# Alternating the two tokens of an output block in PSUM, and storing every other partition

## The chip, the cores and the metric

The kernel runs on one core of a Trainium2 chip. The metric is the time of one execution on the device in microseconds, as the median of several runs. TensorE (PE) does the matrix products into PSUM, ScalarE (ACT) and VectorE (DVE) read PSUM and write SBUF, GpSimd (POOL) works on SBUF alone, and SyncE (SP) issues most DMAs.

## The reference

An efficient attention over 8 batches, 8 heads, 576 tokens and 64 features a head is followed by a multiplicative feed-forward network without a nonlinearity, so that w3 and w_out can be folded into one matrix:

```python
q_s = softmax(q, axis=-1); k_s = softmax(k, axis=2)
kv = einsum('bhsd,bhse->bhde', k_s, v)
attn = einsum('bhsd,bhde->bhse', q_s, kv)
x = attn.transpose(0, 2, 1, 3).reshape(B * S, H * D)      # 4608 x 512
out = (((x @ w1) * (x @ w2)) @ w3) @ w_out                # 4608 x 512, float32
```

## The kernel before, in words

The order of all instructions is a list written out in the file (ORDER), and another list (PICKS) says on which engine a step runs. The steps are recorded in that order, and every engine runs its own share of it as a queue.

**A batch.** q, k and v of one batch lie in SBUF with 128 partitions = 2 groups of heads x 64 token groups; token group p holds the 9 consecutive tokens 9p to 9p + 8, numbered j = 0 to 8. The softmaxes run on ScalarE, VectorE and GpSimd, and kv is a set of small matmuls (L580). The normalised q is transposed, by TensorE or (step qd, L680) by a DMA, into qT, whose columns are ordered by j and then by the 64 groups c.

**The product of q and kv** (prod, L697 to L709). It makes x transposed: features on partitions, tokens along the columns. The first 512 columns (j = 0 to 7) are the main part (tiles named xm, in the pools att, po and pab; the profile names a tile by its pool or by its first use), the last 64 (j = 8) the tail (xt), which is collected over all batches. A matmul here uses a 64x64 quarter of the array: i picks 64 rows of it and one PSUM bank, gg picks 64 columns of it and one half of the partitions. Batches 0 and 1 (SPLIT) make the main part in two halves of 256 columns with two pairs of heads each; batches 2 to 7 make one pair of heads at a time over all 512 columns. The result is scaled and cast to float16 in x by ScalarE or VectorE (xs, L711). The column t of x is token j = t // 64 of group c = t % 64.

**The network.** For a chunk of 512 columns the two up products (L851, or L939 by a seven-product scheme in chunks 6 to 8) are multiplied into ab, and the down product gives 128 tokens x 512 (L873) in chunks 0 and 1. In chunks 2 to 8 (SEVEN) the seven-product scheme (L1029) gives blocks of 2 x 128 tokens and 256 columns. Chunk 8 is the tail of all batches. A block of 128 tokens, number tb, has the columns 128 tb to 128 tb + 127 of x on its partitions: in the first 64 partitions the tokens j = 2 tb of the 64 groups, in the last 64 the tokens j = 2 tb + 1.

**The stores.** The blocks are copied or added into osb (four buffers; in chunks 7 and 8 other tiles that have come free, which the profile names k and v) and stored from there. store (L910) issues two DMAs of 64 partitions x 2 KB for each block of chunks 0 and 1. store_block (L1056) issues two DMAs of 64 partitions x 2 x 1 KB for each block of chunks 2 to 7; in chunk 7 (TWOQ) one of them goes from ScalarE's queue, all others from SP's. For chunk 8 it issues DMAs of all 128 partitions. A buffer of osb is given back when its stores have landed.

Of the kernel before, what the change touches and what calls it, by code (L numbers as in the profile page):

```python
# [265 lines left out]
def kernel(  # L266
# [11 lines left out]
    nc = tc.nc  # L278
    B, H, S, D = q.shape
# [7 lines left out]
    HALF = P // G  # L287
    HH = H // G
    NHP = HH // 2
    NJ = S // HALF  # L290
# [27 lines left out]
    def p_att(shape, dtype, name):  # L318
        return att_pool.tile(shape, dtype, tag="att", name=name)
# [5 lines left out]
    st = {}  # L325
# [195 lines left out]
    def attention(b):  # L521
# [119 lines left out]
        def qeps(p, eng):  # L641
            rr = st["qr", b][:, :, slice(*PARTS[p])]
            if eng == "ACT":
                nc.scalar.activation(out=rr, in_=rr, func=AF.Identity, bias=epst[:, 0:1])
            else:
                return [dve.tensor_scalar_add(out=rr, in0=rr, scalar1=EPS)]
# [35 lines left out]
        def toks(i, hp, gg, j0, j1):  # L682

            return st["qT", b].rearrange("p (j a) (g c) -> p j a g c", a=NHP, g=G)[
                i * D:(i + 1) * D, j0:j1, hp, gg, :]

        def xtile():
            if ("x", b) not in st:
                st["x", b] = work.tile([P, N_CT, MAIN], F16, tag="x", name="x", bufs=NX)
            return st["x", b]  # L690

        def XRING(name):
            if name[1] < XMS:
                return "att"
            return "pab" if name[0] == "xt" else "po" if name[2] else "att"

        def prod(name, hp_list, j0, j1, dst):  # L697
            n = (j1 - j0) * HALF
            for i in range(2):
                bank = {"att": lambda: p_att([P, 512], F32, name[0]), "po": p_o, "pab": p_ab}[XRING(name)]()  # L700
                st[(*name, i)] = bank[:, 0:len(hp_list) * n].rearrange("p (a n) -> p a n", n=n)
            for a, hp in enumerate(hp_list):
                for i in range(2):
                    for gg in range(G):
                        nc.tensor.matmul(  # L705
                            st[(*name, i)][gg * D:(gg + 1) * D, a, :].rearrange(
                                "p (j c) -> p j c", c=HALF),
                            lhsT=st["kv2", b][i * D:(i + 1) * D, hp, gg, :],
                            rhs=toks(i, hp, gg, j0, j1), start=True, stop=True)  # L709

        def xs(name, i, dst, eng):  # L711
            scale(eng, dst(), st[(*name, i)], SC)
# [22 lines left out]
        for p in parts:  # L735
            n = (PARTS[p][1] - PARTS[p][0]) * HH * D
# [6 lines left out]
              lambda eng, p=p: qeps(p, eng), [("qsm", b, p)])  # L743
# [24 lines left out]
        if len(SUBS[b]) == 2:  # L768
            for h in range(2):
                name = ("xm", b, h)  # L770
                dst = lambda i, h=h: xtile()[:, i::2, h * 256:(h + 1) * 256]
                A(name, "PE", 0.22, lambda name=name, h=h: prod(name, [0, 1], 4 * h, 4 * h + 4, None),
                  kvs + qready(h) + free, takes=XRING(name), slots=2, slack=SLACK)
                for i in range(2):
                    A(("xs", b, h, i), moves(512), 0,
                      lambda eng, name=name, i=i, dst=dst: xs(name, i, lambda: dst(i), eng), [name],
                      gives=[name])
            last = [("xm", b, 1)]
            XS[b] = [[("xs", b, h, i) for i in range(2)] for h in range(2)]
        else:  # L780
            for hp in hps:
                name = ("xm", b, hp)
                A(name, "PE", 0.22, lambda name=name, hp=hp: prod(name, [hp], 0, NM, None),
                  kvs + qready(0) + qready(1) + free, takes=XRING(name), slots=2, slack=SLACK)
                for i in range(2):
                    A(("xs", b, hp, i), moves(512), 0,
                      lambda eng, name=name, i=i, hp=hp: xs(
                          name, i, lambda: xtile()[:, 2 * hp + i:2 * hp + i + 1, :], eng),
                      [name], gives=[name])
            last = [("xm", b, hp) for hp in hps]  # L790
            XS[b] = [[("xs", b, hp, i) for hp in hps for i in range(2)]]
        A(("xt", b), "PE", 0.07, lambda: prod(("xt", b), [0, 1], NM, NJ, None), last + qready(1),
          takes=XRING(("xt", b)), slots=2, slack=SLACK)
        for i in range(2):
            A(("xts", b, i), moves(128), 0,
              lambda eng, i=i: xs(("xt", b), i, lambda: xtail[:, i::2, b * HALF:(b + 1) * HALF], eng),
# [40 lines left out]
    def chunk(c):  # L837
# [68 lines left out]
        def os2(tb, c0, c1, eng):  # L906
            st["osb", c, tb, c0] = obuf(c1 - c0)
            copy(eng, st["osb", c, tb, c0], st["po", c, tb, c0][:, 0:c1 - c0])

        def store(tb):  # L910
            for i in range(2):
                b, j = c, 2 * tb + i
                nc.sync.dma_start(
                    out=out[b * S:(b + 1) * S, :].rearrange("(p j) c -> p j c", j=NJ)[:, j, :],
                    in_=st["osb", c, tb][i * HALF:(i + 1) * HALF, :])

        def x_sum(i, eng):
            x0, x1 = [x()[:, 0:2, t:t + 256] for t in (0, 256)], [x()[:, 2:4, t:t + 256] for t in (0, 256)]
            b11, b12, b21, b22 = x0[0], x0[1], x1[0], x1[1]
            s = xsums(c)  # L920
            in0, in1 = {1: (b12, b11), 2: (b22, s[0]), 3: (b22, b12), 4: (b21, s[1])}[i]
            return [engine[eng].tensor_tensor(out=s[i - 1], in0=in0, in1=in1, op=ALU.subtract)]
# [79 lines left out]
        def sums_of(i, eng):  # L1002
            a = st["ab", c]
            a11, a12, a21, a22 = [a[:, 4 * f:4 * f + 4, 256 * t:256 * t + 256]
                                  for t in range(2) for f in range(2)]
            in0, in1, op = {1: (a21, a22, ALU.add), 2: (mine[0], a11, ALU.subtract),
                            3: (a11, a21, ALU.subtract), 4: (a12, mine[1], ALU.subtract)}[i]
            return [engine[eng].tensor_tensor(out=mine[i - 1], in0=in0, in1=in1, op=op)]  # L1008
# [47 lines left out]
        def store_block(n, part=None, z=None):  # L1056
            t0, c0 = n // 10 - 1, (n % 10 - 1) * 256
            if part is not None:
                (nc.sync if part else nc.scalar).dma_start(
                    out=out.rearrange("(t p j) c -> p t j c", p=P, j=NJ)[  # L1060
                        :, 2 * t0 + part, NM, c0:c0 + 256],
                    in_=st["osb", c, n][:, 256 * part:256 * part + 256])
                return
            if c == B:
                nc.sync.dma_start(
                    out=out.rearrange("(t p j) c -> p t j c", p=P, j=NJ)[
                        :, 2 * t0:2 * t0 + 2, NM, c0:c0 + 256],
                    in_=st["osb", c, n].rearrange("p (t x) -> p t x", t=2))
                return
            for i in range(2) if z is None else (z,):  # L1070
                j = 4 * t0 + i
                (nc.scalar if z else nc.sync).dma_start(
                    out=out[c * S:(c + 1) * S, :].rearrange("(p j) c -> p j c", j=NJ)[
                        :, j:j + 3:2, c0:c0 + 256],
                    in_=st["osb", c, n][i * HALF:(i + 1) * HALF, :].rearrange(
                        "p (t x) -> p t x", t=2))

        A = plan.add
        nf = len(SUBS[c])
# [7 lines left out]
        if c in UPS + UP1:  # L1087
# [15 lines left out]
            for i, needs in ((1, []), (2, [("xd", c, 1)]), (3, []), (4, [("xd", c, 2)])):  # L1103
                A(("xd", c, i), {"POOL": (1.06, True), "DVE": (0.39, True)}, 0,
                  lambda eng, i=i: x_sum(i, eng), needs + xn + held)
            for g in range(2):
                for one in kinds:
                    k = lambda i: ("vk", one, c, g, i)
                    p = lambda i: ("vp", one, c, g, i)
# [12 lines left out]
                    for n, needs, gives in (  # L1122
# [8 lines left out]
                        b = ("bs", c, sub, u)  # L1131
# [33 lines left out]
        if c in SEVEN:  # L1165
# [8 lines left out]
            for i, needs in ((3, lo), (1, lo + hi), (2, [("sa", c, 1)]), (4, [("sa", c, 2)])):  # L1174
                A(("sa", c, i), {"POOL": (1.9, True), "DVE": (0.69, True)}, 0,
                  lambda eng, i=i: sums_of(i, eng), needs + last)
# [42 lines left out]
        for sub in range(nf):  # L1219
            for tb in range(4):  # L1220
# [18 lines left out]
                for c0, c1 in zip(cuts, cuts[1:]):  # L1239
# [4 lines left out]
                      lambda eng, tb=tb, c0=c0, c1=c1: os2(tb, c0, c1, eng), [("down", *it)] + gone,  # L1244
# [6 lines left out]
    def weight_sum(i, eng):  # L1251
        b11, b12, b21, b22 = [W3O[:, 4 * f:4 * f + 4, 256 * x:256 * x + 256]
                              for f in range(2) for x in range(2)]
        in0, in1 = {1: (b12, b11), 2: (b22, sums[0]), 3: (b22, b12), 4: (b21, sums[1])}[i]
        return [engine[eng].tensor_tensor(out=sums[i - 1], in0=in0, in1=in1, op=ALU.subtract)]

    for i, needs in ((1, []), (2, [("sT", 1)]), (3, []), (4, [("sT", 2)])):
        plan.add(("sT", i), {"POOL": (1.9, True), "DVE": (0.69, True)}, 0,
                 lambda eng, i=i: weight_sum(i, eng),
# [48 lines left out]
```

## Time and profile before

| what | value |
|---|---|
| median of 3 runs | 230.78 us (230.62 to 231.79) |
| the profiled execution | 231.41 us |
| its span, first to last instruction | 229.6 us |
| granted TensorE clock | 1.000 |
| DMA packets | 42201, 46.56 MB |
| of them under 512 B | 17088 |
| HBM written | 9.44 MB |

The span is what the rows of the profile cover; the rest of the execution's time lies around it. In rows of groups the columns are the source line, engine, operation, output and inputs with their shapes, then the count, the busy time in us, the mean of one in ns and the idle time of the engine ahead of it. Matmuls overlap in TensorE's pipeline, so the duration of one is longer than the distance from its start to the next.

### The profile page before, as it was taken

How to read it: one execution, taken by the hardware profiler on the slowest of the kernel's cores; microseconds unless marked ns; L12 is line 12 of the kernel's file. 1: busy time of each engine (PE TensorE's matmuls, PEld its weight loads, DVE VectorE, ACT ScalarE, POOL GpSimd, SP SyncE). 2: the span in 40 equal slices, each digit the busy share in tenths (PEclk: the TensorE clock that was granted, in tenths of full speed). 3: DMA queues.
4: the chain of work that ended last, by engine and by line, in shares of the span. 5: the costliest groups of instructions: out<-in, count | busy, mean ns of one | idle time of the engine just before them, and what ended most of it. 6: DMA issues, size and time to landing. Idle time of an engine off the chain costs nothing.

```text
span 229.6 us, 5583 instructions
## 1 busy us (share of the span) xinstructions
PE 220.3 (96%) x2239; PEld 149.1 (65%) x2239; DVE 202.6 (88%) x313; ACT 146.4 (64%) x277; POOL 144.1 (63%) x93
## 2 busy tenths in 40 slices
PE   7789999999999999999999999999999999999993
PEld 2345658765857635345665665664788788888882
DVE  1997769989897999999999899899989999899982
ACT  0536865479964899968947889448578453344521
POOL 8233337909999987994895895643099335638200
PEclk9999999999999999999999999999999999999999
DMA  6999999999999979999892866872803430041537
GB/s 201 219 310 210 294 264 264 312 382 295 394 311 215 358 259 222 283 302 301 246 386 76 179 139 176 330 150 47 183 3 76 97 74 1 3 91 27 113 91 229
DMA packets 42201, 46.56 MB, mean 203 GB/s; under 512 B 17088, under 2 KB 29888, under 8 KB 42176
## 3 DMA queue, kind: packets, MB, share of 16 engines
q1 hardware_dynamic: 33920, 33.82, 53.0%
q0 software_dynamic: 7536, 11.73, 21.8%
q10 hardware_dynamic: 720, 0.66, 1.0%
q8 instruction: 17, 0.28, 0.5%
q14 instruction: 8, 0.07, 0.1%
HBM read 38.80 MB, written 9.44 MB: 210 GB/s over the span
## 4 chain that ended last, share of the span: by engine, by line
PE 72%; DMA 22%; issue 1%; POOL 1%; ACT 1%; DVE 0%; POOLq 0%; ACTq 0%
PE pab L851 27%; PE po L1029 16%; PE pg L939 9%; PE pab L939 7%; DMA q<-in_q_dram 6%; DMA k<-in_k_dram 6%; PE po L873 6%; DMA w1sb<-in_moe_w_dram 5%; DMA v<-in_v_dram 4%; PE pab L1029 2%; PE pkv L580 2%; PE xm L705 1%; POOL w L450 1%; PE po L705 0%; POOL wosb L450 0%
## 5 line engine op out<-in xcount | busy, mean ns | idle before, releaser
L851 PE MATMUL pab<-x,w1sb 128*128 128x256 f16 (+1 forms) x256 | 49.5, 326 | 0.3 <-DMA w1sb<-in_moe_w_dram 0.3
L851 PE MATMUL pab<-x,w2sb 128*128 128x256 f16 (+1 forms) x256 | 49.5, 326 | 0.0
L555 POOL TENSOR_TENSOR k<-k,cb 128x1152 f32<-128x1152 f32 x13 | 34.1, 2634 | 14.7 <-DVE w L1008 8.6
L851 PEld LDWEIGHTS <-w1sb 128*128 128x128 f16 x256 | 24.5, 98 | 15.1 <-DMA w1sb<-in_moe_w_dram 0.6
L851 PEld LDWEIGHTS <-w2sb 128*128 128x128 f16 x256 | 24.2, 98 | 15.2 <-issue 1.1
L866 DVE TENSOR_TENSOR ab<-pab,bsb 128x512 f16<-128x512 f32 x48 | 31.8, 676 | 2.0 <-ACT bsb L366 1.2
L625 POOL TENSOR_TENSOR q<-q,qm 128x1280 f32<-128x1280 f32 (+1 forms) x13 | 27.8, 2144 | 4.8 <-issue 2.3
L366 ACT CAST bsb<-pab 128x512 f16<-128x512 f32 x37 | 21.7, 585 | 12.6 <-PE pab L851 12.1
L657 POOL TENSOR_TENSOR en<-eq,qr 128x1024 f16<-128x1024 f16 (+1 forms) x12 | 25.4, 2124 | 6.5 <-ACT bsb L366 5.0
L620 DVE TENSOR_REDUCE qm<-q 128x20 f32<-128x1280 f32 (+1 forms) x16 | 21.3, 1339 | 3.9 <-DMA q<-in_q_dram 3.9
L638 DVE TENSOR_REDUCE qr<-eq 128x20 f32<-128x1280 f16 (+1 forms) x16 | 21.5, 1341 | 1.6 <-ACT eq L633 1.5
L633 ACT ACTIVATE eq<-q 128x1280 f16<-128x1280 f32 (+1 forms) x16 | 18.6, 1167 | 5.3 <-DVE q L625 3.9
L1029 PEld LDWEIGHTS <-w 128*128 128x128 f16 x192 | 18.6, 98 | 4.1 <-issue 0.4
L532 DVE TRANSPOSE_TENSOR_REDUCE kt<-k 128x72 f32<-128x2304 f32 x8 | 20.6, 2570 | 0.1
L366 ACT COPY q<-pg 128x512 f32<-128x512 f32 x19 | 10.8, 586 | 13.9 <-PE pg L939 7.7
L1029 PEld LDWEIGHTS <-ab 128*128 128x128 f16 x168 | 16.4, 98 | 3.5 <-issue 0.2
L563 ACT ACTIVATE ek<-k 128x1152 f16<-128x1152 f32 x16 | 18.3, 1165 | 0.0
L1029 PE MATMUL po<-w 128*128 128x256 f16 x144 | 18.0, 273 | 0.0
L1008 POOL TENSOR_TENSOR w<-ab 128x1024 f16<-128x1024 f16 x5 | 10.6, 2125 | 9.7 <-PE pg L939 3.7
L501 PE MATMUL po<-wosb,w3T 128*128 128x512 f16 x64 | 15.3, 379 | 0.6 <-DMA wosb<-in_moe_w_out_dram 0.5
L873 PE MATMUL po<-W3O,ab 128*128 128x512 f16 x64 | 15.1, 379 | 0.5 <-ACT osb L366 0.5
L366 ACT CAST v<-v 128x1152 f16<-128x1152 f32 x12 | 13.6, 1156 | 2.0 <-DMA v<-in_v_dram 2.0
(145 smaller groups left out, 425.2 us busy)
## 6 DMA issues: line engine op xcount, KB each, us to landing
out_dram<-osb SPq DMA_DIRECT2D x56, 128.0 KB, 2.6
q<-in_q_dram SPq DMA_DIRECT2D x5, 1152.0 KB, 8.0
v<-in_v_dram SPq DMA_DIRECT2D x5, 1152.0 KB, 7.2
k<-in_k_dram SPq DMA_DIRECT2D x4, 1152.0 KB, 9.5
k<-in_k_dram POOLq DMA_DIRECT2D x3, 1152.0 KB, 14.3
v<-in_v_dram POOLq DMA_DIRECT2D x1, 1152.0 KB, 14.0
q<-in_q_dram SPq DMA_DIRECT2D x2, 576.0 KB, 5.8
k<-in_k_dram SPq DMA_DIRECT2D x2, 576.0 KB, 5.0
```

What stands on the lines that cost most here:

```text
L366: return [(nc.scalar.copy if eng == "ACT" else engine[eng].tensor_copy)(out=out, in_=in_)]
L532: dve.tensor_reduce(out=st["kt", b].rearrange("p h j e -> p (h j e)"), in_=kb.rearrange("p h j (e c) -> p (h j e) c", c=QD), axis=AX.X, op ...
L555: return [engine[eng].tensor_tensor(out=kb[:, two(hp), :, :], in0=kb[:, two(hp), :, :], in1=st["cb", b][:, two(hp), None, :].broadcast_to( ...
L620: dve.tensor_reduce(out=st["qm", b][:, :, j], in_=qb[:, :, j, :], axis=AX.X, op=ALU.max)
L625: return [engine[eng].tensor_tensor(out=qb[:, :, j, :], in0=qb[:, :, j, :], in1=st["qm", b][:, :, j, None].broadcast_to([P, HH, n, D]), op ...
L638: dve.tensor_reduce(out=st["qr", b][:, :, slice(*PARTS[p])], in_=st["eq", b, p], axis=AX.X, op=ALU.add)
L657: return [engine[eng].tensor_tensor(out=st["en", b][:, j, :, :].rearrange("p j h d -> p h j d"), in0=st["eq", b, p], in1=st["qr", b][:, :, ...
L851: nc.tensor.matmul(st["p", one, c, sub, u][:, a * (t1 - t0):(a + 1) * (t1 - t0)], lhsT=w[:, ct, fb * P:(fb + 1) * P], rhs=x()[:, ct, t0:t1 ...
L866: dve.tensor_tensor(out=st["ab", c][:, nf * u:nf * u + nf, t0:t1], in0=cut(st["p", 0, c, sub, u]), in1=cut(st["bsb", c, sub, u]), op=ALU.mult)
L873: nc.tensor.matmul(st["po", c, tb], lhsT=st["ab", c][:, ft, tb * P:(tb + 1) * P], rhs=W3O[:, ft, :], start=(ft == 0), stop=(ft == N_FT - 1))
L939: nc.tensor.matmul(st["pg", one, c, g, bank][:, a * 256:a * 256 + 256], lhsT=t[:, c0 + ct, f:f + P], rhs=r[:, r0 + ct, t0:t0 + 256], start ...
L1029: nc.tensor.matmul(to, lhsT=t[:, f0 + ft, t0 + tb * P:t0 + tb * P + P], rhs=r[:, g0 + ft, c0:c0 + 256], start=fresh and (tb == 0 or wide_) ...
```

## The change

TensorE's main products write the columns of a block in another order. Of each four values of j (4h to 4h + 3), j = 4h + 2z + t goes to block 2h + t, and there to the partitions 2c + z. So a block holds the tokens j and j + 2 of the 64 groups alternating, one token of a group on the even partition and the other on the odd one. In PSUM the 64 columns of one j, which were side by side, are 2 fp32 elements apart; the moving operand is read as before, and a matmul's output, 64x512 before, has the form 64x2x2x128 (64x2x128 for the halves of 256). The tail products are written as before.

The stores follow: one DMA takes the even partitions of a block and one the odd ones, in place of the first 64 and the last 64. In store_block the two tokens of a DMA are now j and j + 1, where they were j and j + 2. The sizes, the number of DMAs and the queues stay. On all five engines the instructions stand in the same order as before.

```diff
@@ prod
                     for gg in range(G):
+                        to = st[(*name, i)][gg * D:(gg + 1) * D, a, :]
                         nc.tensor.matmul(
-                            st[(*name, i)][gg * D:(gg + 1) * D, a, :].rearrange(
-                                "p (j c) -> p j c", c=HALF),
+                            to.rearrange("p (j c) -> p j c", c=HALF) if name[0] == "xt" else
+                            to.rearrange("p (h t c z) -> p h z t c", t=2, z=2, c=HALF),
                             lhsT=st["kv2", b][i * D:(i + 1) * D, hp, gg, :],
                             rhs=toks(i, hp, gg, j0, j1), start=True, stop=True)
@@ store
-            for i in range(2):
-                b, j = c, 2 * tb + i
+            for z in range(2):
+                j = tb // 2 * 4 + tb % 2 + 2 * z
                 nc.sync.dma_start(
-                    out=out[b * S:(b + 1) * S, :].rearrange("(p j) c -> p j c", j=NJ)[:, j, :],
-                    in_=st["osb", c, tb][i * HALF:(i + 1) * HALF, :])
+                    out=out[c * S:(c + 1) * S, :].rearrange("(p j) c -> p j c", j=NJ)[:, j, :],
+                    in_=st["osb", c, tb][z::2, :])
@@ store_block
-            for i in range(2) if z is None else (z,):
-                j = 4 * t0 + i
-                (nc.scalar if z else nc.sync).dma_start(
+            for z, queue in ((0, nc.sync), (1, nc.sync)) if z is None else ((z, (nc.sync, nc.scalar)[z]),):
+                j = 4 * t0 + 2 * z
+                queue.dma_start(
                     out=out[c * S:(c + 1) * S, :].rearrange("(p j) c -> p j c", j=NJ)[
-                        :, j:j + 3:2, c0:c0 + 256],
-                    in_=st["osb", c, n][i * HALF:(i + 1) * HALF, :].rearrange(
-                        "p (t x) -> p t x", t=2))
+                        :, j:j + 2, c0:c0 + 256],
+                    in_=st["osb", c, n][z::2, :].rearrange("p (t x) -> p t x", t=2))
```

## The prediction

> **What bounds the kernel now.** I read the busy shares first, then the same by stage, then what TensorE waits for, then the chain that ended last, and only then the lines that the change touches. The page gives the shares of the whole span:
>
> ```profile
> PE 220.3 (96%) x2239; PEld 149.1 (65%) x2239; DVE 202.6 (88%) x313; ACT 146.4 (64%) x277; POOL 144.1 (63%) x93
> ```
>
> An average hides stages, so the next view cuts the span. Its columns are the stretch, its length, then busy time and count of each engine, the granted clock, the share of the 16 DMA engines and GB/s:
>
> ```profile
> 31.00:46.00 15.00, 14.66 (x139) 11.21 (x139) 13.70 (x18) 7.33 (x16) 12.34 (x9) 1.00 1.30 278
> 46.00:100.00 54.00, 53.18 (x566) 31.35 (x565) 49.39 (x72) 44.63 (x85) 45.67 (x23) 1.00 1.01 307
> 100.00:160.00 60.00, 60.00 (x604) 35.65 (x603) 56.98 (x87) 44.94 (x94) 41.52 (x19) 1.00 0.75 207
> 160.00:226.00 66.00, 65.82 (x667) 56.69 (x664) 60.45 (x108) 33.29 (x60) 31.57 (x20) 1.00 0.34 75
> ```
>
> From 46 to 226 us TensorE is busy 179.0 of 180.0 us, at the full clock. The DMA engines are full up to 100 us (1.01), then 0.75, then 0.34. Full DMA engines alone would not bound; what decides is whether TensorE waits for them. All of TensorE's waits from 46 us on:
>
> ```profile
> PE po L873 <- ACT osb L366: 0.5, 1, 0.5
> PE pab L851 <- DMA w1sb<-in_moe_w_dram: 0.3, 1, 0.3
> PE xm L705 <- DMA qT<-en: 0.3, 1, 0.3
> PE po L1029 <- ACT x L370: 0.2, 1, 0.2
> ```
>
> Four waits, 1.3 us together. No wait for a store stands here. So a transfer that becomes faster can give back part of 1.3 us at most, while every 0.1 us more of TensorE's own work in this stretch moves the end by nearly 0.1 us. The chain of waits says the same at its end (start, length, what):
>
> ```profile
> 92.31 1.73 PE pab L851 x8
> ...
> 95.19 0.34 PE xm L705 x4
> 95.53 0.22 PE po L705 x4
> ...
> 145.12 0.87 PE po L1029 x8
> ...
> 222.51 3.09 PE pab L1029 x28
> ```
>
> L705, the matmuls that the change alters, stands in it as a link of its own.
>
> **The change, part 1: TensorE's writes.** No instruction is added, removed or moved on any engine; the order of all five is the same. What differs on TensorE is where the columns of L705 land: in the main products two neighbouring columns of the moving operand now land two fp32 elements (8 bytes) apart in PSUM instead of side by side. The tail products (xt) keep their form. How many there are, from the view of L705:
>
> ```profile
> L705 PE MATMUL xm<-qT,kv x60: 267/293/401, 31.1 to 182.1; 64*64 64x256 f16 x32, 64*64 64x512 f16 x28
> ...
> L705 PE MATMUL xt<-qT,kv x24: 192/203/214, 34.6 to 94.0; 64*64 64x64 f16 x24
> L705 PE MATMUL po<-qT,kv x20: 372/389/400, 95.4 to 181.8; 64*64 64x512 f16 x20
> ```
>
> That is 48 matmuls of 512 columns (28 + 20) and 32 of 256. They do not cost their durations one after another: each takes a 64x64 quarter of the array, and the four of a set run together. The timeline shows two such sets:
>
> ```profile
> 95.12 0.41 PE L705 MATMUL xm<-qT,kv 64*64 64x512 f16 x4
> 95.36 0.39 PE L705 MATMUL po<-qT,kv 64*64 64x512 f16 x4
> ```
>
> The four of the first start in one merged row at 95.12 and the next set starts 0.24 us later. A full-array matmul of 512 columns takes 1.73 / 8 = 0.216 us in the chain's row at 92.31, one of 256 columns 0.87 / 8 = 0.109 us in the row at 145.12. So a set costs one pass of its columns, and there are 12 sets of 512 (6 batches of 2) and 8 sets of 256 (batches 0 and 1).
>
> Nothing in this trace writes PSUM from TensorE with a step, so the price has to be bounded. From below: a column costs what it costs now, 0.216 / 512 = 0.42 ns, and the price is nothing. From above I take the other engines that touch PSUM, one element of each partition at a time:
>
> ```profile
> L366 ACT COPY osb<-po 128x512 f32<-128x512 f32 x10 | 5.9, 585 | 2.9 <-PE po L1029 2.9
> L370 ACT ACTIVATE xtail<-pab 128x128 f16<-128x128 f32 x8 | 2.0, 282 | 0.0
> L366 DVE COPY osb<-po 128x512 f32<-128x512 f32 x3 | 2.1, 687 | 1.2 <-PE po L873 0.7 <-PE po L1029 0.6
> L372 DVE TENSOR_SCALAR xtail<-pab 128x128 f16<-128x128 f32 x2 | 0.6, 283 | 0.0
> ```
>
> The slope between 128 and 512 elements is (585 - 282) / 384 = 0.79 ns an element on ScalarE, and (687 - 283) / 384 = 1.05 ns on VectorE. TensorE puts a value into each partition every 0.42 ns, about twice as fast as either. The simplest reading is that TensorE's neighbours go in as a pair, and that a value whose neighbour goes elsewhere takes the place of a pair. Then a set takes two passes. That lies nearest to ScalarE's 0.79 ns (0.79 / 0.42 = 1.9), and it is the value that I take:
>
> - 12 sets x 0.216 = 2.59 us; 8 sets x 0.109 = 0.87 us; together 3.46 us more of TensorE.
> - At ScalarE's slope: 12 x (0.404 - 0.216) + 8 x (0.202 - 0.109) = 3.0 us. At VectorE's: 12 x (0.538 - 0.216) + 8 x (0.269 - 0.109) = 5.1 us. These and zero are the ends.
>
> Behind a longer set stand the casts to x on ScalarE and VectorE, which wait for it, and the next matmuls in TensorE's queue, which have no other work to hide it: TensorE was busy through. Only the waits can absorb something. The 0.3 us for w1sb ends with a weight load, and the transposed load of qT with a DMA behind the softmax; neither is timed by TensorE, so both absorb what reaches them: 0.6. The 0.5 us for ScalarE's osb is the open one. ScalarE's queue ahead of it:
>
> ```profile
> 79.26 1.16 ACT L366 CAST v<-v 128x1152 f16<-128x1152 f32 x1 [0.63 <-DMA v<-in_v_dram]
> ...
> 80.32 0.58 ACT L366 CAST bsb<-pab 128x512 f16<-128x512 f32 x1
> ...
> 81.97 0.57 ACT L366 COPY osb<-po 128x512 f32<-128x512 f32 x1
> ```
>
> The cast of v is timed by a load, the cast bsb takes a product from TensorE, and osb stands behind both; so the wait may move along with TensorE (absorbs 0) or stay (absorbs 0.5); I take half. The 0.2 us for x comes right behind L705 itself and moves with it: 0. Net: 3.46 - 0.6 - 0.25 = **2.6 us**, with 2.2 (all 1.3 absorbed) and 2.9 as its own ends.
>
> [...]
>
> **Part 2: the stores.** Each 128 KB store reads 64 partitions, before as one half, now as every other one; the number of DMAs, their bytes and their runs in DRAM stay. What the store packets cost shows in two windows of the DMA view, the first from 201 to 204 us with half-partition stores alone, the second from 226.00 to 228.25 us with the last stores, over 128 partitions (packets, MB, share of 16 engines):
>
> ```profile
> q1 hardware_dynamic: 568, 0.52, 82.5%
> ```
>
> ```profile
> q1 hardware_dynamic: 623, 0.60, 79.8%
> q10 hardware_dynamic: 144, 0.13, 17.8%
> ```
>
> 0.825 x 16 x 3 us / 568 = 70 ns a packet against 0.976 x 16 x 2.25 us / 767 = 46 ns. If every other partition gives the second figure, a store of 128 packets takes 0.37 us of the 16 engines instead of 0.56. What is that worth? When the stores are issued, from the view of osb:
>
> ```profile
> L1072 SPq DMA_DIRECT2D out_dram<-osb x40: 595/602/652, 124.5 to 212.3; - x40
> L913 SPq DMA_DIRECT2D out_dram<-osb x16: 512/595/2826, 51.5 to 114.1; - x16
> ```
>
> The 40 run after 124 us, where the DMA engines have a share of 0.75 and less and nobody waits for a store; SP itself needs 0.60 us to issue one, longer than either figure: 0 us. The 16 earlier ones (whole rows of 2 KB) share full DMA engines with loads; what they free can come back only through the 1.3 us of waits. The tail stays: the chain runs on matmuls to 225.6 us, then the last VectorE block and the last stores, which belong to the tail chunk and are not changed. I take 0, with -0.8 (the qT and osb waits gone) as the lower end.
>
> [...]
>
> **Sum.** The profiled execution took 231.41 us with a span of 229.6. Its sum is 231.41 + 2.6 = 234.0. The median of the runs is 230.78, 0.63 below that execution, so I forecast 230.78 + 2.6 = **233.4**.
>
> **Rivals.**
> - **The step is free.** TensorE's write keeps its 0.42 ns whatever the address. For it: nothing in the trace shows a stepped write to be slow, and the pair is an inference from other engines. Then nothing remains: 230.8, within 230.4 to 231.2.
> - **The other side: faster.** The step is free, and the lighter stores let loads land earlier between 46 and 100 us, so that the qT wait and the osb wait go: 0.3 + 0.5 = 0.8 us, 230.0. Against it: those waits end with a transpose behind the softmax and with ScalarE, whose queue held a cast of v that a load released; only that one has a DMA behind it. It decides only if the step costs less than 0.8 us in all, which is 0.05 us for a set of 512.
> - **A stepped value costs as much as on VectorE** (1.05 ns). 5.1 - 0.85 = 4.3 us: 235.1. For it: it is the slowest access of PSUM in the trace. Against it: ScalarE does better on the same banks.
> - **A partial price**, some set-up per set rather than per column: between 231.2 and 232.6.
>
> **How the numbers follow.** Two passes (with ScalarE's slope) 0.60, its own range 232.8 to 233.8; free 0.25; faster 0.05; VectorE's price 0.06; partial 0.04. A measurement of this kernel tells about 0.5% (1.15 us) from no change. Free lies within it, and so does a quarter of partial (0.01): same 0.26. Faster: I leave its whole 0.05, though it reaches only 230.0. Slower: 0.60 + 0.06 + 0.03 = 0.69. The range goes from 230.3, which takes in the free case, to 235.1, the upper bound of the unknown price.
>
> **What would show it.** If I am right, the start of the second set of L705 moves from 0.24 to about 0.45 us behind the first, the chain's 0.34 + 0.22 for a batch becomes about 1.0, the durations of the 512 forms go from 390 to about 600 ns while xt keeps its 203, the waits for w1sb and qT vanish, and the last matmul ends 2.6 us later than now. The half-partition stores show about 46 ns a packet and nobody is earlier for it. If the sets keep their 0.24, the step is free and the forecast is wrong in its first term. If the sets double and the end does not move, the error is in what the waits absorb. If waits for a load appear or vanish by more than 0.8 us, part 2 was misjudged.

## The result, and the profile after

The changed kernel takes 233.18 us (median of 6 runs, 232.93 to 233.74) against 230.74 us for the kernel before in the same comparison. The ratio is 1.0102, 95% interval 1.0081 to 1.0124: 2.4 us slower, 1.9 to 2.9. The profiled execution took 233.22 us with a span of 231.4.

The page's first line, of the kernel after: TensorE has 3.1 us more of busy time, no other engine has moved by more than 0.5 us.

```profile
PE 223.4 (97%) x2239; PEld 149.5 (65%) x2239; DVE 202.8 (88%) x313; ACT 146.9 (63%) x277; POOL 144.0 (62%) x93
```

The same cut into stretches (length, then busy time and count of each engine, granted clock, share of the DMA engines, GB/s):

```profile
31.00:46.00 15.00, 15.00 (x138) 11.22 (x137) 13.22 (x18) 6.75 (x16) 11.52 (x9) 1.00 1.30 279
46.00:100.00 54.00, 54.00 (x568) 31.34 (x566) 49.83 (x72) 45.36 (x86) 46.13 (x23) 1.00 0.98 309
100.00:160.00 60.00, 60.00 (x599) 35.22 (x597) 56.33 (x86) 43.96 (x92) 41.84 (x19) 1.00 0.69 203
160.00:226.00 66.00, 66.00 (x659) 56.28 (x658) 60.75 (x107) 34.17 (x62) 31.55 (x20) 1.00 0.24 70
```

TensorE is now busy without a gap from 31 to 226 us: the four waits of before, 1.3 us, are gone, and the list of its waits after 46 us is empty. The DMA engines have less to do after 100 us (0.69 and 0.24, before 0.75 and 0.34), and nobody gained by it.

The lines that the change altered. First the groups of L706 (the old L705), durations in ns as min/median/max:

```profile
L706 PE MATMUL xm<-qT,kv x60: 373/418/631, 31.5 to 183.8; 64*64 64x256 f16 x32, 64*64 64x512 f16 x28
...
L706 PE MATMUL xt<-qT,kv x24: 192/203/213, 35.4 to 93.9; 64*64 64x64 f16 x24
L706 PE MATMUL po<-qT,kv x20: 586/613/631, 95.4 to 183.4; 64*64 64x512 f16 x20
```

The 512-column form went from a median of 389 to 613 ns, 224 more, which is about one more pass of 512 columns (216); xt, whose write was not changed, stands at 203 as before. Durations overlap (below, the first set's row lasts to 95.60 and the second starts at 95.39), so what counts is the starts. The timeline of batch 3's two sets, and of the next product in the queue:

```profile
94.98 0.62 PE L706 MATMUL xm<-qT,kv 64*64 64x512 f16 x4
95.39 0.64 PE L706 MATMUL po<-qT,kv 64*64 64x512 f16 x4
95.97 0.82 PE L852 MATMUL pab<-x,w2sb 128*128 128x512 f16 x3
```

From the first set to the next product it is 0.99 us; before, the same three starts were 95.12, 95.36 and 95.68, 0.56 us. A batch costs 0.43 us more, 0.213 us a set in the unrounded starts. The chain of waits has the same links, only longer:

```profile
95.05 0.55 PE xm L706 x4
95.61 0.43 PE po L706 x4
...
224.32 3.08 PE pab L1030 x28
```

Its last link begins at 224.32 where it began at 222.51, 1.81 us later; that is the whole difference of the two profiled executions (233.22 - 231.41 = 1.81). What comes behind it, the last blocks and stores, takes as long as before. The medians differ by 2.4 us, more than these two executions, because the profiled one of the kernel before lies 0.67 us above its median and that of the kernel after at its own.

### The profile page after: what moved, and what is told of

Same layout as the page of the kernel before. It is cut to its first block, busy times and chain, and to the rows that moved or that the text cites. A ratio compares the mean times of both kernels' runs of the same rounds, so it can differ in the third digit from the quotient of the medians.

```text
span 231.4 us, 5583 instructions
## 1 busy us (share of the span) xinstructions
PE 223.4 (97%) x2239; PEld 149.5 (65%) x2239; DVE 202.8 (88%) x313; ACT 146.9 (63%) x277; POOL 144.0 (62%) x93
## 4 chain that ended last, share of the span: by engine, by line
PE 87%; DMA 10%; DVE 0%; issue 0%; POOL 0%; POOLq 0%
PE pab L852 37%; PE po L1030 16%; DMA w<-in_moe_w_dram 10%; PE pg L940 9%; PE pab L940 7%; PE po L874 6%; PE pkv L580 2%; PE pab L1030 2%; PE xm L706 2%; PE po L501 2%; PE po L706 1%; PE w3t L489 1%; DVE v L1050 0%; PE pab L706 0%; PE qtp L672 0%
## 5 line engine op out<-in xcount | busy, mean ns | idle before, releaser
L366 ACT COPY kept<-po 128x512 f32<-128x512 f32 x17 | 10.0, 588 | 6.5 <-PE po L1030 6.4
```

The lines of the kernel that those rows point to most:

```text
L366: return [(nc.scalar.copy if eng == "ACT" else engine[eng].tensor_copy)(out=out, in_=in_)]
```

## The experiments

Every ratio is to the kernel before, on the same chip. Two theories stood at the start. A: TensorE's write takes two passes whenever neighbours do not go in side by side, its waits absorb 1.3 us of the sum, and the stores are worth nothing. B: the lighter stores gave something back, so that the write alone would cost more than the whole change.

**The write alone.** The change's prod, the kernel before for all the rest.

> Only TensorE's stepped write; the stores take the two halves of a block as before (so the token rows of the output are permuted). Theory A (the write takes two passes, the stores are worth nothing): 3.4 us more of TensorE, 1.3 us absorbed by waits, so 2.1 to 2.6 us slower than the kernel before, the same as the whole change within 0.3 us. Rival B (the lighter stores gave something back in the whole change, by bringing the load of v earlier): slower than the whole change by 0.4 to 0.8 us, so 2.8 to 3.2 us slower than before, and the wait of TensorE for osb near 82 us is still there.

Measured: 233.10 us, ratio 1.0104 (1.0088 to 1.0120), the same as the whole change (1.0102). TensorE waits for nothing from 46 us on here either, so the wait for osb is gone without the new stores. By the ratios the two differ by 0.05 us, give or take about 0.6: of B's 0.4 to 0.8 the upper end is out, the lower one is not.

**The stores alone.** prod as before, with the change's store and store_block.

> Only the stores of every other partition; TensorE writes as before (so the token rows of the output are permuted). Theory A: the same time as before within 0.3 us, store packets at 46 ns instead of 70. Rival B: 0.4 to 0.8 us faster than before, with TensorE's wait for osb near 82 us shorter or gone.

Measured: 230.85 us against 230.82, ratio 0.9999 (0.9982 to 1.0016). No gain and no loss, within 0.4 us. The wait for osb is missing in this profile, as B said; but it is missing as well in the profiles of the pairs and of batches 3 to 6 below, which have the old stores and the old time of every write up to that point. So it comes and goes with the execution, and tells nothing about the stores. That the stores themselves became lighter is plain in the DMA view, here two windows of 3.5 us (202.5 to 206) with four stores each, the write alone with half-partition stores first, then the whole change with every other partition (packets, MB, share of 16 engines):

```profile
q1 hardware_dynamic: 576, 0.52, 71.4%
```

```profile
q1 hardware_dynamic: 576, 0.52, 44.8%
```

0.714 x 16 x 3.5 us / 576 = 69 ns a packet against 0.448 x 16 x 3.5 us / 576 = 44 ns, in about the same time for the group: SP issued these four stores in 2.55 us, one per 0.65 us, in the kernel before (from 200.08) as in the changed one (from 201.89). The median from issue to landing fell from 2.6 us (the kernel before and the write alone) to 2.2 (the whole change). Nothing gains from either: in the lists of waits of the kernel before and of the changed one, none ends with one of these stores.

**Pairs.** Neighbours stay together, pairs 16 bytes apart:

```diff
-                            to.rearrange("p (h t c z) -> p h z t c", t=2, z=2, c=HALF),
+                            to.rearrange("p (k z y) -> p z k y", z=2, y=2),
```

> As the write alone, but two neighbouring columns stay side by side and the pairs are 4 elements (16 bytes) apart; stores as before (so the token rows of the output are permuted). Theory A (neighbours go into PSUM as a pair): a set of 512 columns keeps 0.21 us, the time is that of the kernel before within 0.5 us. Rival C (any output that is not one contiguous run costs): sets at 0.43 us, 2 to 3 us slower than before.

Measured: 230.97 us, ratio 1.0009 (0.9994 to 1.0024). The sets of batch 3:

```profile
94.53 0.41 PE L706 MATMUL xm<-qT,kv 64*64 64x512 f16 x4
94.77 0.39 PE L706 MATMUL po<-qT,kv 64*64 64x512 f16 x4
```

0.24 us apart, as before the change. The output is as scattered as in the change, in runs of two values, and the sets cost no more. Rival C falls: in these runs it is not contiguity of the whole that matters but of two neighbours (0.24 us with them side by side, 0.41 without). Nor is it the number of nested steps in the output's form, which is larger here than in the next run.

**A longer step.**

```diff
-                            to.rearrange("p (h t c z) -> p h z t c", t=2, z=2, c=HALF),
+                            to.rearrange("p (c z) -> p z c", c=HALF),
```

> As the write alone, but with a step of 4 or 8 elements (16 or 32 bytes) in place of 2; stores as before (so the token rows of the output are permuted). Theory A (a value without its neighbour takes the place of a pair, wherever it goes): sets of 512 at 0.43 us as with step 2, 2 to 3 us slower than before. Rival D (the price grows with the distance): sets at 0.6 us or more, 4 us slower or more.

Measured: 233.44 us, ratio 1.0123 (1.0099 to 1.0148). The sets:

```profile
95.18 0.62 PE L706 MATMUL xm<-qT,kv 64*64 64x512 f16 x4
95.59 0.64 PE L706 MATMUL po<-qT,kv 64*64 64x512 f16 x4
```

0.41 us as with step 2. In the halves of 256 columns the step is 4 here, and the median of the 60 matmuls xm, which falls among these 32, is 418 ns as with step 2 (293 before). So 8, 16 and 32 bytes cost the same here; D falls.

**Where the sum is paid.** The stepped write in batches 3 to 6 alone, then in batches 0 to 2 alone:

```diff
+                            to.rearrange("p (j c) -> p j c", c=HALF) if name[0] == "xt" or b not in (3, 4, 5, 6) else
```

> The stepped write in batches 3 to 6 alone, 8 sets of 512; stores as before (so the token rows of these batches are permuted). Theory A (TensorE's added work is absorbed only where it waited before, and between 90 and 180 us it never waited): 8 x 0.213 = 1.7 us slower, all of it at the end. Rival E (later work shifts and takes part of it back in the last batches): 0.8 us slower or less.

Measured: 232.26 us, ratio 1.0061 (1.0046 to 1.0076), 1.4 us (1.1 to 1.75). E is out, and 1.7 lies within the interval, at its edge. The profile is sharper than the time, because executions differ by some tenths ahead of 80 us. I count from the down product at 82 us, where the kernel before waits last for a long time, to the last link of the chain. Before, and batches 3 to 6 (timeline and chain of each):

```profile
82.59 1.24 PE L873 MATMUL po<-W3O,ab 128*128 128x512 f16 x5 [0.49 <-ACT osb L366]
```

```profile
81.69 1.67 PE L874 MATMUL po<-W3O,ab 128*128 128x512 f16 x7
...
223.28 3.08 PE pab L1030 x28
```

222.51 - 82.59 = 139.92 us before, 223.28 - 81.69 = 141.59 here: 1.67 more for 8 sets, 0.21 a set. Nothing is absorbed in this stretch.

```diff
+                            to.rearrange("p (j c) -> p j c", c=HALF) if name[0] == "xt" or b not in (0, 1, 2) else
```

> The stepped write in batches 0, 1 and 2 alone, 8 sets of 256 and 2 of 512; stores as before (so the token rows of these batches are permuted). Raw 8 x 0.107 + 2 x 0.213 = 1.3 us more of TensorE. Theory A: the waits near 46, 73 and 82 us absorb it, so 0 to 0.4 us slower. Rival E: the absorption lies elsewhere (the last batch, the tail), so 0.9 to 1.3 us slower.

Measured: 231.06 us against 230.89, ratio 1.0019 (1.0000 to 1.0038), 0.4 us (0 to 0.9) of the raw 1.3. Its profile:

```profile
82.19 1.03 PE L874 MATMUL po<-W3O,ab 128*128 128x512 f16 x4
...
222.14 3.08 PE pab L1030 x28
```

222.14 - 82.19 = 139.95, as before (139.92): all of it was over by 82 us. By the times, 0.9 us (0.4 to 1.3) of the 1.3 was absorbed, as A said; E's 0.9 us slower lies just outside the interval. The profiles cannot size it better. From the first set near 31 us to the product at 82 us it is 51.0 us here, but 51.5 in the profiled execution before, 50.8 with pairs and 50.6 with batches 3 to 6 alone, and these three pay nothing in that stretch.

**Is it this write, or any?** The step moved to the down products of chunks 0 and 1, full-array matmuls that accumulate:

```diff
-                nc.tensor.matmul(st["po", c, tb], lhsT=st["ab", c][:, ft, tb * P:(tb + 1) * P],
+                nc.tensor.matmul(st["po", c, tb].rearrange("p (k z) -> p z k", z=2),
+                                 lhsT=st["ab", c][:, ft, tb * P:(tb + 1) * P],
```

> The step of 2 elements moved to other matmuls: the 64 down products of chunks 0 and 1 (128x128 array, 512 columns, accumulating over 8), all else as before (so the output's columns of these chunks are permuted). Theory A (the price belongs to the write into PSUM, not to quarter-array matmuls or to first writes): starts at 0.43 us in place of 0.216, 64 x 0.213 = 13.6 us more of TensorE, 12.5 to 13.6 us slower. Rival I (a full array or an accumulation hides or multiplies it): starts at 0.22 us and no change, or 0.6 us and more.

Measured: 243.94 us, ratio 1.0556 (1.0510 to 1.0601), 12.8 us. Eight of these matmuls take 3.43 us in the chain, before 1.73, so 0.429 us each in place of 0.216; I is out. Before, then here:

```profile
65.37 1.73 PE po L873 x8
```

```profile
48.09 3.43 PE po L873 x8
```

**The same order without a stepped write.** First by the read of the moving operand (j + 4 in place of j + 2, with the stores to match):

```diff
+                            to.rearrange("p (t c z) -> p t c z", z=2, c=HALF),
...
+                            rhs=read if name[0] == "xt" else
+                            read.rearrange("p (z t) c -> p t c z", z=2), start=True, stop=True)
```

> The tokens of a block alternate as in the change, with j and j + 4 in batches 2 to 7, but the order is made by the read of the moving operand from SBUF (inner step 256 or 512 fp16 elements) and PSUM is written in one contiguous run; the stores take every other partition. Theory A (it is the write into PSUM that costs): sets of 512 at 0.21 us, within 0.5 us of the kernel before. Rival F (any stepped stream of TensorE costs, a read as much as a write): sets at 0.43 us or more, 2 us slower or more.

Measured: 233.81 us, ratio 1.0124 (1.0106 to 1.0142). Here theory A's narrow form fails: PSUM is written in one run, and the set is slower still.

```profile
95.12 0.67 PE L707 MATMUL xm<-qT,kv 64*64 64x512 f16 x4
95.62 0.65 PE L707 MATMUL po<-qT,kv 64*64 64x512 f16 x4
```

0.50 us between the sets. This read, which jumps with each fp16 value, costs more than the stepped write does (0.41). F holds. The step of this read, by the layout of qT (256 elements from one j to the next), is 1024 elements in batches 2 to 7 and 512 in batches 0 and 1, not the 512 and 256 of the expectation. Shorter steps, and runs of two or more fp16 values, were not run, so what makes the read dear stays open.

Then by the cast:

```diff
+            if name[0] != "xt":
+                to = to.rearrange("p a (u z) -> p a z u", z=2)
+                read = read.rearrange("p a (z u) -> p a z u", z=2)
             scale(eng, to, read, SC)
```

> The same block order made by the cast from PSUM to x on ScalarE and VectorE, which reads contiguously and writes fp16 values 4 bytes apart; TensorE as before, the stores take every other partition. Theory A: ScalarE's cast stays near 0.60 us and VectorE's near 0.69, the time is that of the kernel before within 0.5 us. Rival G (a stepped write costs there too): casts at 0.8 us or more and TensorE waiting for x.

Measured: 231.48 us, ratio 1.0022 (1.0009 to 1.0035), 0.5 us slower. The casts, busy time in us and mean in ns, before and then here:

```profile
L370 ACT ACTIVATE x<-xm 128x512 f16<-128x512 f32 x18 | 10.2, 599 | 3.8 <-PE xm L705 3.6
...
L372 DVE TENSOR_SCALAR x<-xm 128x512 f16<-128x512 f32 x4 | 2.7, 685 | 2.1 <-PE xm L705 2.1
```

```profile
L370 ACT ACTIVATE x<-xm 128x512 f16<-128x512 f32 x18 | 12.7, 748 | 3.4 <-PE xm L705 3.4
...
L372 DVE TENSOR_SCALAR x<-xm 128x512 f16<-128x512 f32 x4 | 2.9, 727 | 2.2 <-PE xm L705 2.2
```

ScalarE's cast went from 599 to 748 ns, between the two expectations, VectorE's from 685 to 727. It is the cheapest of the three places for the order. As G said, TensorE waits for x:

```profile
34.90 0.92 PE L855 MATMUL pab<-x,w2sb 128*128 128x256 f16 x7 [0.61 <-ACT x L370]
183.17 1.03 PE L1033 MATMUL po<-W3O,ab 128*128 128x256 f16 x8 [0.31 <-ACT x L370]
```

Before, the second of these waits was 0.18 us and the first did not exist. The first is not the length of a cast. The products at 34.90 read the first 256 columns of x, and they wait for the casts of the other 256, which start at 34.11 and 34.15; before, the same products ran beside those casts and waited for no semaphore. So the new form of the cast's output brought a wait on columns that the products do not read. Whether the 0.5 us comes from that wait or from the longer casts is not shown. No version came out faster than the kernel before.

## Why the prediction was right

It forecast 233.4; measured were 233.2.

- **The bound was read rightly.** TensorE's own time in this stretch sets the end: batches 3 to 6 alone add 1.67 us for 8 sets, all of it at the end.
- **The raw sum.** 12 sets x 0.216 + 8 x 0.109 = 3.46 us; measured 0.213 for a set of 512 and half of that for one of 256 (from two such sets to the next product 54.77 to 55.12 before, 54.84 to 55.40 after, 0.21 more for the two), so 3.4 us. The inference behind it, that TensorE's neighbours go in as a pair, was the author's estimate, from other engines' slopes. How the values go in, no run shows. What the runs show is what costs: with pairs 16 bytes apart the sets of batch 3 stayed 0.24 us apart, with single values at a step of 2 or 8 it was 0.41. That the price came out near ScalarE's slope, 0.429 / 512 = 0.84 ns a value against 0.79, is luck as far as these runs go: none connects the two.
- **The absorption fits in size, but not for the reasons given.** The prediction let the waits take 0.85 us. By the times it was 3.4 - 2.4 = 1.0 us (0.5 to 1.5), so 0.85 cannot be told from it. But its list of waits came from one execution, 0.6 us above the median, and the forecast was counted from the median. Two of the four waits, for w1sb and for osb, are not in every execution. All of TensorE's waits from 46 us on with pairs, where its writes cost nothing:

```profile
PE xm L706 <- DMA qT<-en: 0.5, 1, 0.5
PE po L1030 <- ACT x L370: 0.2, 1, 0.2
```

The profile of batches 3 to 6 has the same two, of 0.4 and 0.2 us. The wait for osb in the execution before came with a late load of v: ScalarE idled 0.63 us for it (the prediction's row at 79.26), and it does not in these two. So the half of osb's 0.5 us that the prediction counted was no property of the kernel, and that the sum still fits is luck. The wait for x in batch 7, which was to move along with L705 and absorb 0, is gone after the change. The product at 82 us in the kernel after:

```profile
82.53 1.24 PE L874 MATMUL po<-W3O,ab 128*128 128x512 f16 x5
```

From it to the last link it is 224.32 - 82.53 = 141.79 us, 1.87 more than before. The ten sets of batches 3 to 7 are 2.13 by themselves, so about 0.26 was absorbed there, of which the wait for x is 0.18.
- **The stores were worth 0**, as forecast, for the reason given: no wait of TensorE ends with a store. The half-partition packets took 69 ns and those of every other partition 44, a factor of 1.6 (the prediction had 70 and 46), and the time did not move: 230.85 us with the new stores alone, against 230.82.

## What to carry to other kernels

Before changing how an engine writes so that a transfer runs better, look for the instruction that waits for that transfer; here there was none, and the bill went to the engine that waited 1.3 us in 180. If TensorE has to permute its output, keep two neighbouring fp32 columns together: in these runs pairs left the sets 0.24 us apart, and single values made it 0.41 at steps of 2 and 8 (at a step of 4 the matmuls of 256 columns took 418 ns in place of 293, as at 2) and doubled the full-array matmul, 0.429 us in place of 0.216. Where a busy engine's work grows, add up its idle gaps first: they are what can be absorbed, and here only work ahead of a gap was absorbed by it. Look for the gaps in more than one execution: one that a late load made is not there to be counted on.

## What the runs showed of the hardware

A stepped read of TensorE's moving operand costs as well, and more than the stepped write: 0.50 us from one set of 512 fp16 columns to the next against 0.41, with the values 1024 elements apart. ScalarE writing fp16 values 4 bytes apart took 748 ns for 512 elements in place of 599, VectorE 727 in place of 685. Half-partition stores of 1 KB runs took 69 ns a packet with the write alone, stores of every other partition 44 with the whole change.
